# Fewer, larger loads per pair of heads, with GpSimd placing the last 64 tokens, and the first weights on ScalarE's queue

## The chip, the core and the metric

The kernel runs on one core of one Trainium2 chip. The metric is the device time of one execution in microseconds (us). Of the kernel before there are three timed executions: median 894.34 us, from 890.95 to 898.97. One more execution was profiled; all rows below come from it.

## The reference

Eight batches of 576 tokens pass through three blocks.

```python
# attention with a feature map, per head (8 heads of 64)
def phi(x):
    proj = x @ w_phi                                   # 64 -> 128
    proj = proj - max(abs(proj), axis=-1)
    return concatenate([exp(proj), exp(-proj)])        # 256 features
kv = phi(k).T @ v;  z = sum(phi(k), tokens)
x  = (phi(q) @ kv) / (phi(q) @ z + 1e-6)               # heads side by side: 576 x 512
# causal convolution of 5 taps, gate, two products
gate = sigmoid(conv5(x));  x = (gate * (x @ w_val)) @ w_outA
# gated MLP with a product over tokens
h = relu(x @ w_in);  u, v = h[:, :512], h[:, 512:]
v = layernorm(v);  v = w_spatial @ v + b_spatial
out = (u * v) @ w_out
```

The moe weights w_val, conv_w, w_out and w_out2 are given as 64-bit floats; the kernel loads their two 32-bit words and puts them together itself. It multiplies w_outA by w_in once (the product weights wg and wu), and splits each operand of the large products into a high and a low part, so that one product is three matmuls.

## The kernel before, in words

The program is not written out in the order in which it runs. Each operation is recorded with a key (a place in time, L33 to L36), the buffers it reads and writes, and the engines that may do it. A planner in the kernel (`order`, L222) then plays the engines in a model of its own and writes out an instruction order for each engine: at each moment an engine takes the ready operation with the smallest key. A key may run ahead of the oldest unfinished one by at most WINDOW, 0.405. Buffers come from an arena in SBUF (`fa`, 19152 columns; `ra` for the split operands) and are reused; where a buffer is reused, the instruction that fills it waits for the last user of what lay there. On the chip nothing of the model's times remains: each engine and each queue runs its instructions in the order written, and stops at an instruction whose semaphores have not come.

Work units around the change:

- **Weights** (`weights`, L516). POOL (GpSimd) writes zeros and ones into small tiles, then runs one partition_all_reduce on a tile `warm`. An identity matrix is made in DRAM: `eye` is filled with zeros, then its diagonal with ones, then read back into `ident`. Each 128 rows of a 64-bit weight take one transfer of 512 KB, an absolute value on ScalarE (ACT), four operations on VectorE (DVE) and, for w_val, a copy (ACT) and a subtraction (DVE).
- **A pair of heads** (32 pairs, `attention`, L744). `load_k` and `load_q` (L591, L605) load 512 tokens of k, q and v into arena buffers, and the last 64 tokens of both heads into block-diagonal tiles `k4`, `q4` and `v4` (three of each, used in turn). `project` (L616) makes 12 products on TensorE (PE). `kexp` (DVE, ACT) makes the features of k; `qmax` copies the projected q out of PSUM (ACT) and takes its maximum over partitions (POOL, partition_all_reduce); `kvacc` makes k-features times v, `kvturn` transposes it with `ident`, `num` multiplies by q's features (24 products of 32x288 and those of the denominator), and `divide` (L729) sends the denominators through DRAM (`rden`) and multiplies.
- **A batch** (`mlp`, L788). When the four pairs of a batch are divided, the convolution, the split and the product with `wv` (w_val) begin; `wg`, `wu`, `ws` and `wo` follow.

All transfers are issued by SP (SyncE), in one queue (`dma`, L422). A transfer takes one of eight semaphores in turn, and waits for the transfer that used that semaphore before. Every operation helper has one line (L383 for ACT and DVE, L418 POOL, L428 transfers, L439 and L452 products, L673 transposes), so the rows are told apart by tile names: `fa` is the arena, `ra` the split operands, `bank` PSUM.

Of the kernel before, what the change touches and what calls it, by code (L numbers as in the profile page):

```python
# [12 lines left out]
U32 = mybir.dt.uint32  # L13
# [6 lines left out]
B, H, S, D = 8, 8, 576, 64  # L20
F = 128
DM = 512
# [3 lines left out]
REM = 512  # L26
# [8 lines left out]
W_VAL, W_CONV, W_OUT, W_G, W_U, W_SP, W_OUT2, W_STEP, W_EYE = -1.59, -1.198, -0.852, -0.889, -0.626, -0.225, 0.273, 0.06, -1.334  # L35
M_CONV, M_VAL, M_V, M_U, M_SP, M_OUT, M_ALL = -0.177, -0.295, -0.048, 0.078, 0.002, 0.205, 57.899  # L36
LONG_W, LONG_A, LONG_M = True, False, False
WINDOW = 0.405
# [118 lines left out]
class Op:  # L157
    __slots__ = ("key", "ways", "bufs", "need", "users", "ready", "start", "end", "way", "n", "modes")

# [29 lines left out]
class Plan:  # L189
# [7 lines left out]

    def add(self, ways, reads, writes, modes=(FULL, FULL)):

# [3 lines left out]
        op.key = self.key  # L203
        op.modes = modes
        op.users, op.ready, op.start, op.end, op.way = [], 0.0, None, None, None
# [16 lines left out]
    def order(self, window, hold):  # L222
# [41 lines left out]
        while len(done) < len(ops):  # L264
# [13 lines left out]
            while again:  # L278
# [4 lines left out]
                for e in self.ENGINES:  # L283
# [6 lines left out]
                    for op in ready:  # L290
# [4 lines left out]
                        if e == "PE":  # L295
# [4 lines left out]
                            busy = op.end - now  # L300
                        if e == "SP":
                            transfers = max(transfers, now + busy + 0.63) + until
                            op.end = transfers + 0.85
# [34 lines left out]
def attn_moe_gmlp_kernel(  # L338
# [82 lines left out]

    def dma(out, in_):  # L422
        n = 1
        for d in (out.shape() if isinstance(out, View) else out.shape):
            n *= d

        def run():
            nc.sync.dma_start(out=real(out), in_=real(in_))  # L428

        rows = (out.shape() if isinstance(out, View) else out.shape)[0]  # L430
        plan.add({"SP": (0.475 if rows == 128 else 0.65, 4 * n / 360e3, run)}, views(in_), views(out))

# [27 lines left out]
    def split(src, hi, lo):  # L460

        copy(hi, src)
        sub(lo, src, hi.f32())
# [28 lines left out]

    def load_f64(src, n):

        raw, w = fa.buf(2 * n), fa.buf(n)
        m = 2 * n // len(src)
        for i, x in enumerate(src):
            dma(raw.bitcast(U32)[:, m * i:m * i + m], x.bitcast(U32))
        words = raw.bitcast(U32).rearrange("p (n t) -> p n t", t=2)
# [13 lines left out]
    def rows(ap, k):  # L513
        return ap[128 * k:128 * k + 128]

    def weights():  # L516
# [6 lines left out]
        def fill(x, value):  # L523
            pool(0.1 + cols_of(x) / 960, "memset", x, [], x, value)


        for t in k4 + q4 + v4:
            for hh in range(2):
                fill(t[64 * hh:64 * hh + 64, 64 - 64 * hh:128 - 64 * hh], 0.0)
# [5 lines left out]
        fill(warm, 0.0)  # L535
        pool(9.0, "partition_all_reduce", warm[:, 4:8], [warm], warm[:, 4:8], warm[:, 0:4], channels=128,
             reduce_op=bass_isa.ReduceOp.absmax)
        at(W_EYE)
        zero, one = fa.buf(128), fa.buf(1)
        fill(zero, 0.0)  # L540
        dma(eye, zero)
        fill(one, 1.0)
        dma(eye.rearrange("a b -> (a b)")[0:128 * 128:129].unsqueeze(1), one)
        dma(ident, eye)
# [44 lines left out]
    xt = {}  # L589

    def load_k(P):  # L591
# [21 lines left out]
    def half(hh):  # L613
        return slice(64 * hh, 64 * hh + 64)

    def project(k, kl, q, ql):  # L616
# [6 lines left out]
            for c in range(4) for hh in range(2)  # L623
        ] + [(qas[hh], wphi[half(hh)], q[half(hh)], True, True) for hh in range(2)], FULL, ROWS)
        return kas + [rest[:, 0:F]], [(qas[hh], rest[:, F + 64 * hh:F + 64 * hh + 64]) for hh in range(2)]
# [378 lines left out]
```

## Time and profile before

| | |
|---|---|
| timed executions | 890.95, 894.34, 898.97 us |
| the profiled execution | 895.74 us |
| its span, first to last instruction | 894.0 us |
| PE busy | 846.4 us, 95% |
| DVE, ACT, POOL busy | 694.3, 515.0, 148.1 us |
| mean granted clock of TensorE | 0.988 |
| share of the chain of waits | PE 69%, DVE 13%, DMA 11% |

The span is 1.7 us less than the execution's time. A busy share is a mean over stages; the rows below cut the span where the work changes. A "granted clock" of 1.00 is 2.4 GHz, the other level is 1.2 GHz, and a value between them is a mix of both in that stretch.

### The profile page before, as it was taken

Reading aid. Unit: us, or ns where it says so; the run is one execution under the profiler, and the core shown is the slowest. Engines: PE = TensorE matmul, PEld = TensorE weight load, DVE = VectorE, ACT = ScalarE, POOL = GpSimd, SP = SyncE. Lnnn points to the kernel's source line nnn. Section 1 sums busy time; section 2 is a strip of 40 time slices with the busy share of each in tenths; the row PEclk is TensorE's granted clock in tenths of the full one; section 3 lists DMA queues with packets and bytes.
Section 4 is the critical chain, followed back from the end, with each engine's and each line's share of the span. In section 5 each row is a group of like instructions: output and inputs, shape, how many; then the busy total and the mean of one; then the engine's idle time right before and its main releaser. Section 6 shows DMA issues by size and latency. Waiting matters only on the chain.

```text
span 894.0 us, 19046 instructions
## 1 busy us (share of the span) xinstructions
PE 846.4 (95%) x7312; PEld 671.4 (75%) x7312; DVE 694.3 (78%) x1619; ACT 515.0 (58%) x1097; POOL 148.1 (17%) x129
## 2 busy tenths in 40 slices
PE   3769889899999999999999999999999999999997
PEld 2534468677886887777887888787887888789896
DVE  5888778997877897688778896688878896796541
ACT  3856565575566664576566664576556674543331
POOL 4421210211211120111111120112211110100000
PEclk8999989999999999999999999999999999999999
DMA  5764215130221313131221222130221221010001
GB/s 184 226 180 120 68 27 178 27 88 27 77 66 43 74 38 102 42 89 27 64 81 42 75 65 78 41 88 26 72 73 43 74 65 38 13 46 27 24 7 59
DMA packets 66131, 62.22 MB, mean 70 GB/s; under 512 B 28662, under 2 KB 45430, under 8 KB 66040
## 3 DMA queue, kind: packets, MB, share of 16 engines
q1 hardware_dynamic: 66040, 61.00, 24.3%
q8 instruction: 57, 0.93, 0.4%
q14 instruction: 34, 0.28, 0.1%
HBM read 50.13 MB, written 9.65 MB: 67 GB/s over the span
## 4 chain that ended last, share of the span: by engine, by line
PE 69%; DVE 13%; DMA 11%; ACT 3%; issue 2%; SPq 2%; POOL 0%; DVEq 0%; ACTq 0%; POOLq 0%
PE bank L439 48%; PE bank L452 20%; DVE fa L383 11%; DMA fa<-rden 5%; ACT fa L383 3%; SPq L428 2%; DVE ra L383 1%; DMA fa<-in_w_spT_dram 1%; PE bank L673 1%; DMA rden<-fa 1%; DMA fa<-in_w_out_dram 1%; DMA fa<-in_v_dram 1%; DMA fa<-in_w_val_dram 1%; DMA k<-in_kT_dram 0%; POOL fa L418 0%
## 5 line engine op out<-in xcount | busy, mean ns | idle before, releaser
L383 ACT ACTIVATE fa<-fa 128x576 f32<-128x576 f32 (+2 forms) x445 | 255.1, 628 | 104.6 <-DVE fa L383 72.8
L383 ACT ACTIVATE fa<-bank 128x512 f32<-128x512 f32 (+6 forms) x395 | 162.1, 455 | 162.7 <-PE bank L439 85.6
L418 POOL PARTITION_ALL_REDUCE fa<-fa x64 | 140.6, 2237 | 528.1 <-ACT fa L383 405.1
L383 DVE TENSOR_TENSOR fa<-fa 128x576 f32<-128x576 f32 (+4 forms) x348 | 157.1, 465 | 57.6 <-DMA fa<-rden 29.6
L452 PE MATMUL bank<-fa 128*32 128x288 f32 (+2 forms) x2192 | 164.0, 402 | 3.0 <-DVE fa L383 1.1
L452 PEld LDWEIGHTS bank<-fa 128*32 128x32 f32 (+1 forms) x2192 | 76.0, 112 | 78.2 <-issue 30.7
L383 ACT ACTIVATE ra<-fa 128x256 fp32r<-128x256 f32 (+5 forms) x201 | 87.1, 459 | 82.4 <-DVE fa L383 69.0
L439 PE MATMUL bank<-ws,ra 128*128 128x256 f32 (+1 forms) x768 | 114.7, 298 | 2.5 <-DVE fa L383 2.0
L439 PE MATMUL bank<-wg,ra 128*128 128x512 f32 (+1 forms) x480 | 116.4, 395 | 0.0
L439 PE MATMUL bank<-ra,wu 128*128 128x256 f32 (+1 forms) x768 | 111.6, 301 | 4.9 <-DVE fa L383 3.4
L439 PEld LDWEIGHTS bank<-ra,wu 128*128 128x128 f32 x768 | 105.0, 191 | 13.0 <-issue 5.2
L383 DVE TENSOR_TENSOR ra<-fa,ra 128x256 fp32r<-128x256 f32 (+4 forms) x224 | 103.1, 488 | 13.0 <-ACT ra L383 5.9
L439 PEld LDWEIGHTS bank<-ws,ra 128*128 128x128 f32 x768 | 104.9, 189 | 7.2 <-DVE fa L383 4.2
L439 PEld LDWEIGHTS bank<-ra,wv 128*128 128x128 f32 x768 | 103.0, 189 | 8.5 <-ACT fa L383 4.0
L439 PE MATMUL bank<-ra,wv 128*128 128x256 f32 (+1 forms) x768 | 105.8, 297 | 2.2 <-ACT fa L383 2.2
L383 DVE SCALAR_TENSOR_TENSOR fa<-fa,convw 128x576 f32<-128x576 f32 x128 | 102.9, 823 | 2.4 <-ACT fa L383 2.0
L439 PEld LDWEIGHTS bank<-wg,ra 128*128 128x128 f32 (+1 forms) x480 | 83.7, 179 | 25.7 <-DVE fa L383 1.9
L439 PE MATMUL bank<-wo,ra 128*128 128x512 f32 x432 | 101.6, 391 | 0.2 <-DVE fa L383 0.2
L383 DVE SCALAR_TENSOR_TENSOR fa<-fa 128x576 f32<-128x576 f32 (+4 forms) x192 | 93.8, 496 | 9.1 <-ACT fa L383 6.8
L439 PEld LDWEIGHTS bank<-wo,ra 128*128 128x128 f32 x432 | 80.4, 188 | 18.0 <-issue 0.9
L383 DVE TENSOR_SCALAR fa<-fa 128x2 int32<-128x2 int32 (+8 forms) x192 | 51.3, 284 | 20.1 <-ACT fa L383 14.4
L383 DVE TENSOR_REDUCE fa<-bank 128x4 f32<-128x512 f32 (+1 forms) x96 | 51.0, 548 | 16.3 <-PE bank L452 14.0
(63 smaller groups left out, 614.3 us busy)
## 6 DMA issues: line engine op xcount, KB each, us to landing
fa<-rden SPq DMA_DIRECT2D x64, 144.0 KB
fa<-in_v_dram SPq DMA_DIRECT2D x32, 264.0 KB
fa<-in_qT_dram SPq DMA_DIRECT2D x32, 256.0 KB
fa<-in_kT_dram SPq DMA_DIRECT2D x32, 256.0 KB
out_dram<-fa SPq DMA_DIRECT2D x32, 256.0 KB
fa<-in_w_in_dram SPq DMA_DIRECT2D x8, 512.0 KB
fa<-in_w_val_dram SPq DMA_DIRECT2D x4, 512.0 KB
fa<-in_w_outT_dram SPq DMA_DIRECT2D x4, 512.0 KB
```

What stands on the lines that cost most here:

```text
L383: return lambda: getattr(engine, method)(**{k: real(v) for k, v in kw.items()})
L418: getattr(nc.gpsimd, method)(*(real(a) for a in args), **{k: real(v) for k, v in kw.items()})
L428: nc.sync.dma_start(out=real(out), in_=real(in_))
L439: nc.tensor.matmul(real(acc), lhsT=real(l), rhs=real(r), start=first and i == 0, stop=last and i == n - 1)
L452: nc.tensor.matmul(real(o), lhsT=real(l), rhs=real(r), start=first, stop=last)
L673: nc.tensor.transpose(real(tp)[:, F * s:F * s + F], real(kvT)[:, F * s:F * s + F], real(ident))
```

## The change

Per pair, SP now issues four transfers instead of nine: q whole (576 tokens), k whole, v of 512 tokens, and v's last 64 tokens once for both halves of the partitions (`vt`, a broadcast). Six copies of 64x64 on POOL (`place`) put the last tokens into `k4`, `q4` and `v4`. The buffers of k and q grow from 512 to 576 columns. The four transfers of w_val and the three of `eye` and `ident` go to ACT's queue. The fills of POOL stand in another order, with the tiles of pair 0 and `warm` first. Eleven keys have other values, and attention's buffers are taken from the upper end of the arena (LONG_A).

```diff
-AK_LOAD, AK_PROJ, AK_ACC, AK_SUM, AK_TURN = -0.401, 0.095, 0.584, 0.308, 2.416
-AQ_LOAD, AQ_MAX, AQ_EXP, AQ_NUM, AQ_HEAD, A_DIV = -0.902, 0.399, 1.995, 3.059, 1.055, 5.005
+AK_LOAD, AK_PROJ, AK_ACC, AK_SUM, AK_TURN = -0.44, 0.095, 0.595, 0.308, 2.337
+AQ_LOAD, AQ_MAX, AQ_EXP, AQ_NUM, AQ_HEAD, A_DIV = -0.852, 0.399, 2.005, 3.059, 1.055, 5.031
...
-LONG_W, LONG_A, LONG_M = True, False, False
+LONG_W, LONG_A, LONG_M = True, True, False
...
-    def dma(out, in_):
+    def dma(out, in_, engine="SP"):
...
-            nc.sync.dma_start(out=real(out), in_=real(in_))
+            (nc.sync if engine == "SP" else nc.scalar).dma_start(out=real(out), in_=real(in_))
...
+        zero, one = fa.buf(128), fa.buf(1)
+        fill(zero, 0.0)
+        fill(one, 1.0)
+        for i in range(3):
+            for t in (k4[i], q4[i], v4[i]):
+                for hh in range(2):
+                    fill(t[64 * hh:64 * hh + 64, 64 - 64 * hh:128 - 64 * hh], 0.0)
+            if not i:
+                fill(warm, 0.0)
+                at(-1.99)
+                pool(9.0, "partition_all_reduce", warm[:, 4:8], [warm], warm[:, 4:8], warm[:, 0:4], channels=128,
+                     reduce_op=bass_isa.ReduceOp.absmax)
...
-        dma(eye, zero)
+        dma(eye, zero, "ACT")
...
-            split(load_f64([rows(w_val, k)], DM), wv[0][k], wv[1][k])
+            split(load_f64([rows(w_val, k)], DM, "ACT"), wv[0][k], wv[1][k])
...
+    def place(out, in_):
+        pool(0.2, "tensor_copy", out, [in_], out, in_)
+
     def load_k(P):
         b, hp = divmod(P, NP)
-        k = fa.buf(REM)
-        dma(k, kT[b, hp, :, 0:REM])
+        k, vt = fa.buf(S), fa.buf(2 * VW)
+        dma(k, kT[b, hp, :, 0:S])
         v = fa.buf(4 * 2 * VW)
         dma(v.rearrange("p (c d) -> p c d", c=4), v1[b, 0:REM, hp].rearrange("(c p) d -> p c d", p=128))
+        dma(vt, v1[b, REM:S, hp].unsqueeze(0).to_broadcast([2, 64, 2 * VW]))
         kl, vl = k4[P % 3], v4[P % 3]
         for hh in range(2):
-            r = slice(64 * hh, 64 * hh + 64)
-            dma(kl[r, r], kT[b, hp, r, REM:S])
-            dma(vl[r, r], v1[b, REM:S, hp, (2 * VW - D) * hh:(2 * VW - D) * hh + D])
+            r = half(hh)
+            place(kl[r, r], k[r, REM:S])
+            place(vl[r, r], vt[r, (2 * VW - D) * hh:(2 * VW - D) * hh + D])
...
     def load_q(P):
         b, hp = divmod(P, NP)
-        q, ql = fa.buf(REM), q4[P % 3]
-        dma(q, qT[b, hp, :, 0:REM])
+        q, ql = fa.buf(S), q4[P % 3]
+        dma(q, qT[b, hp])
         for hh in range(2):
-            dma(ql[half(hh), half(hh)], qT[b, hp, half(hh), REM:S])
+            place(ql[half(hh), half(hh)], q[half(hh), REM:S])
```

What the planner makes of it stands in the order of the built programs. The engines' first instructions are the first place. SP, before (the loads of pair 0; `k_0`, `q_0`, `v_0` are its block-diagonal tiles; DMAHW is another transfer's semaphore):

```order
L428 DMA wphi<-in_w_phi_dram 128x1x128
L428 DMA fa<-in_qT_dram 128x512
L428 DMA q_0_82<-in_qT_dram 64x64 x2
L428 DMA fa<-in_w_val_dram 128x1024
L428 DMA fa<-in_kT_dram 128x512
L428 DMA fa<-in_v_dram 128x4x132
L428 DMA k_0_79<-in_kT_dram 64x64
```

and SP, changed:

```order
L428 DMA wphi<-in_w_phi_dram 128x1x128
L428 DMA fa<-in_qT_dram 128x576
L428 DMA fa<-in_kT_dram 128x576 [waits DVE_49]
L428 DMA fa<-in_v_dram 128x4x132
L428 DMA fa<-in_v_dram 128x1x132
L428 DMA fa<-in_qT_dram 128x576 [waits DMAHW0_49]
L428 DMA fa<-in_kT_dram 128x576 [waits DMAHW2_49]
```

The load of k of pair 0 has been given columns that the first block of w_val used; the value it waits for is DVE's fifth instruction, the subtraction that ends that block. Everything of SP after it, the loads of v and of pair 1 among them, stands behind it.

ACT, changed (before, no transfer stood here: the table load was followed by the absolute value and the copy `wv_0`, and the first copies of `bank_70` and `bank_67` were its fifth and sixth ACTIVATE):

```order
L428 DMA fa<-in_w_val_dram 128x1024
L383 ACT_TABLE_LOAD
L383 ACTIVATE fa<-fa 128x512 [waits DMAHW0_49]
L383 ACTIVATE wv_0_99<-fa 128x512 [waits DVE_49]
L428 DMA fa<-in_w_val_dram 128x1024 [waits Activation_49]
L428 DMA fa<-in_w_val_dram 128x1024
L428 DMA fa<-in_w_val_dram 128x1024 [waits DMAHW1_49]
L428 DMA eye<-fa 128x128 [waits DMAHW3_49,Pool_49]
L428 DMA eye<-fa 128x1 [waits DMAHW3_49,DMAHW0_49,Pool_49]
L383 ACTIVATE fa<-fa 128x512
```

The last row is the absolute value of the second block of w_val. It now stands behind two transfers of `eye`: the first waits until the second block of w_val has landed, the second until the first has landed in DRAM and until q of pair 1 has landed. On POOL, the copies into `k_0` wait for the load of k.

The second place is PE ahead of the first product with `wv` (batch 0). Before, the end of pair 5's kvacc, the products of `num` of pair 4, a transpose, and then `wv`:

```order
L452 MATMUL bank_67<-fa,v_2_87 128x256
L452 MATMUL bank_67<-fa 32x256 x16
L452 MATMUL bank_67<-fa,ones 32x128 x4
L452 MATMUL bank_67<-fa,mine_89 32x128 x2
L452 MATMUL bank_67<-fa,mine_90 32x128 x2
L452 MATMUL bank_70<-fa 32x288 x8
L452 MATMUL bank_71<-fa 32x288 x8
L452 MATMUL bank_73<-fa 32x288 x8
L673 MATMUL bank_67<-ident,fa 128x128 x3
L439 MATMUL bank_67<-ra,wv_0_99 128x256
```

Changed, `num` of pair 3 (the last that batch 0 needs), with kvacc of pair 4 and the last weight products (128x512) behind it; after these come only the 12 products of pair 5's projection, and then `wv`:

```order
L452 MATMUL bank_68<-fa 32x288 x8
L452 MATMUL bank_71<-fa 32x288 x8
L452 MATMUL bank_73<-fa 32x288 x8
L452 MATMUL bank_69<-fa 128x512 x4
L452 MATMUL bank_67<-fa,v_1_86 128x256
L452 MATMUL bank_67<-fa 32x256 x16
L452 MATMUL bank_67<-fa,ones 32x128 x16
L452 MATMUL bank_67<-fa,mine_89 32x128 x2
L452 MATMUL bank_67<-fa,mine_90 32x128 x2
L452 MATMUL bank_69<-fa 128x512 x4
L452 MATMUL bank_67<-fa 128x512 x4
L452 MATMUL bank_68<-fa 128x512 x4
```

Counted in the built programs: before, 464 products of PE stand ahead of the first with `wv`, now 397; `num` of pair 3 stood behind 147 DVE instructions, now behind 114; the first `wv` product behind 168, now 158. At PE's 661st product both orders stand at the same place, the third group of `wu` of batch 0; 233 DVE instructions are needed for it before, 223 now, and 238 for the group of `wg` behind it.

## Rows read from the trace of the kernel before

**Rows 1.** Windows: stretch, us, busy PE, PEld, DVE, ACT, POOL, PEclk, DMA share, GB/s

```profile
0.00:20.00 20.00, 4.37 (x25) 3.32 (x26) 10.24 (x15) 6.71 (x12) 10.20 (x35) 0.91 0.64 201
20.00:64.00 44.00, 32.47 (x448) 19.57 (x449) 38.56 (x70) 30.14 (x69) 14.32 (x8) 0.93 0.67 192
64.00:108.00 44.00, 43.07 (x307) 21.67 (x310) 38.26 (x68) 26.50 (x54) 8.55 (x6) 1.00 0.38 108
108.00:160.00 52.00, 41.88 (x378) 33.13 (x369) 40.23 (x87) 30.82 (x66) 9.39 (x7) 0.93 0.31 91
...
200.00:889.00 689.00, 685.57 (x5795) 565.33 (x5794) 529.74 (x1286) 392.16 (x838) 101.23 (x70) 1.00 0.20 54
```

**Rows 2.** Waits of PE, first 160 us: us in total, times, longest

```profile
PE bank L452 <- DMA k<-in_kT_dram: 15.6, 2, 9.5
```

**Rows 3.** Timeline of SP's queue: start, us, what [idle before, releaser]

```profile
3.18 0.58 SPq L428 DMA_DIRECT2D fa<-in_w_val_dram  x1
...
5.96 0.59 SPq L428 DMA_DIRECT2D k<-in_kT_dram  x1
...
7.23 1.53 SPq L428 DMA_DIRECT2D fa<-in_w_val_dram  x3
...
14.48 3.20 SPq L428 DMA_DIRECT2D eye<-fa  x2
17.73 0.47 SPq L428 DMA_DIRECT2D k<-in_kT_dram  x1
```

**Rows 4.** Chain of waits within the first 30 us: start, us, what

```profile
7.23 4.57 DMA fa<-in_w_val_dram
```

**Rows 5.** Waits of SP's queue, first 30 us

```profile
SPq L428 <- DMA eye<-fa: 2.5, 1, 2.5
```

**Rows 6.** Timeline of ACT

```profile
7.07 0.66 ACT L383 ACTIVATE fa<-fa 128x512 f32<-128x512 f32 x1 [5.06 <-DMA fa<-in_w_val_dram]
...
13.81 1.32 ACT L383 ACTIVATE fa<-bank 128x512 f32<-128x512 f32 x4
```

**Rows 7.** Timeline of DVE

```profile
7.76 0.89 DVE L383 TENSOR_SCALAR fa<-fa 128x512 f32<-128x512 f32 x2 [7.76 <-ACT fa L383]
...
10.80 0.69 DVE L383 TENSOR_TENSOR wv<-fa,wv 128x512 fp32r<-128x512 f32 x1 [0.70 <-ACT wv L383]
12.59 0.89 DVE L383 TENSOR_SCALAR fa<-fa 128x512 f32<-128x512 f32 x2 [1.09 <-ACT fa L383]
...
15.06 1.52 DVE L383 TENSOR_SCALAR fa<-fa 128x512 uint32<-128x512 uint32 x1
...
19.40 1.27 DVE L383 TENSOR_REDUCE fa<-bank 128x4 f32<-128x512 f32 x2
...
112.79 0.69 DVE L383 TENSOR_TENSOR fa<-fa 128x512 f32<-128x512 f32 x1 [4.74 <-ACT fa L383]
```

**Rows 8.** Groups of POOL by shape: busy us, mean ns of one, idle before

```profile
L418 POOL PARTITION_ALL_REDUCE fa<-fa x64 | 140.6, 2237 | 528.1 <-ACT fa L383 405.1 <-DVE fa L383 76.4 <-DMA out_dram<-fa 17.7
...
L418 POOL MEMSET k<- 64x64 f32 x6 | 0.9, 146 | 0.5 <-POOLq L988 0.3
```

**Rows 9.** Timeline of PE

```profile
9.53 0.77 PE L452 MATMUL bank<-wphi,k 128*128 128x128 f32 x2 [9.53 <-DMA k<-in_kT_dram]
...
19.86 0.77 PE L452 MATMUL bank<-wphi,k 128*128 128x128 f32 x2 [6.10 <-DMA k<-in_kT_dram]
...
25.65 0.67 PE L452 MATMUL bank<-fa,v 128*128 128x256 f32 x2 [1.61 <-issue]
...
63.84 7.10 PE L452 MATMUL bank<-fa 128*128 128x512 f32 x16 [1.08 <-DVE fa L383]
...
105.45 3.09 PE L452 MATMUL bank<-fa 128*32 128x288 f32 x48
...
127.33 11.30 PE L439 MATMUL bank<-ra,wv 128*128 128x256 f32 x84 [2.04 <-ACT fa L383]
...
159.26 2.56 PE L439 MATMUL bank<-ra,wu 128*128 128x256 f32 x12 [2.28 <-DVE fa L383]
```

More of the change, by code (lines that the diff above doesn't have):

```diff
@@ L157 @@
 class Op:
-    __slots__ = ("key", "ways", "bufs", "need", "users", "ready", "start", "end", "way", "n", "modes")
+    __slots__ = ("key", "ways", "bufs", "need", "users", "ready", "start", "end", "way", "n", "modes", "dma")
 def cols_of(x):
@@ L196, in __init__, with add @@
         self.key = 0.0
-    def add(self, ways, reads, writes, modes=(FULL, FULL)):
+    def add(self, ways, reads, writes, modes=(FULL, FULL), dma=False):
         op = Op()
@@ L203, in add @@
         op.key = self.key
-        op.modes = modes
+        op.modes, op.dma = modes, dma
         op.users, op.ready, op.start, op.end, op.way = [], 0.0, None, None, None
@@ L427, in run @@
         def run():
-            nc.sync.dma_start(out=real(out), in_=real(in_))
+            (nc.sync if engine == "SP" else nc.scalar).dma_start(out=real(out), in_=real(in_))
         rows = (out.shape() if isinstance(out, View) else out.shape)[0]
-        plan.add({"SP": (0.475 if rows == 128 else 0.65, 4 * n / 360e3, run)}, views(in_), views(out))
+        plan.add({engine: (0.475 if rows == 128 else 0.65, 4 * n / 360e3, run)}, views(in_), views(out), dma=True)
     def gemm(acc, terms, first=True, last=True):
@@ L490, in attn_moe_gmlp_kernel, with load_f64 @@
     ws = wtiles("ws", 4, S)
-    def load_f64(src, n):
+    def load_f64(src, n, engine="SP"):
         raw, w = fa.buf(2 * n), fa.buf(n)
@@ L524, in fill @@
             pool(0.1 + cols_of(x) / 960, "memset", x, [], x, value)
-        for t in k4 + q4 + v4:
-            for hh in range(2):
-                fill(t[64 * hh:64 * hh + 64, 64 - 64 * hh:128 - 64 * hh], 0.0)
+        zero, one = fa.buf(128), fa.buf(1)
[10 more added lines that the diff above has]
+                     reduce_op=bass_isa.ReduceOp.absmax)
         fill(ones, 1.0)
@@ L533, in weights @@
                 fill(mine[hh][64 * r:64 * r + 64], float(r == hh))
-        fill(warm, 0.0)
-        pool(9.0, "partition_all_reduce", warm[:, 4:8], [warm], warm[:, 4:8], warm[:, 0:4], channels=128,
-             reduce_op=bass_isa.ReduceOp.absmax)
         at(W_EYE)
-        zero, one = fa.buf(128), fa.buf(1)
-        fill(zero, 0.0)
-        dma(eye, zero)
-        fill(one, 1.0)
-        dma(eye.rearrange("a b -> (a b)")[0:128 * 128:129].unsqueeze(1), one)
-        dma(ident, eye)
+        dma(eye, zero, "ACT")
+        dma(eye.rearrange("a b -> (a b)")[0:128 * 128:129].unsqueeze(1), one, "ACT")
+        dma(ident, eye, "ACT")
         for x, value in ((s2, 1.0), (wr2, 0.0)):
@@ L589, in attn_moe_gmlp_kernel, with half @@
     xt = {}
+    def half(hh):
+        return slice(64 * hh, 64 * hh + 64)
+    def place(out, in_):
+        pool(0.2, "tensor_copy", out, [in_], out, in_)
     def load_k(P):
         b, hp = divmod(P, NP)
-        k = fa.buf(REM)
-        dma(k, kT[b, hp, :, 0:REM])
+        k, vt = fa.buf(S), fa.buf(2 * VW)
+        dma(k, kT[b, hp, :, 0:S])
         v = fa.buf(4 * 2 * VW)
         dma(v.rearrange("p (c d) -> p c d", c=4), v1[b, 0:REM, hp].rearrange("(c p) d -> p c d", p=128))
+        dma(vt, v1[b, REM:S, hp].unsqueeze(0).to_broadcast([2, 64, 2 * VW]))
         kl, vl = k4[P % 3], v4[P % 3]
         for hh in range(2):
-            r = slice(64 * hh, 64 * hh + 64)
-            dma(kl[r, r], kT[b, hp, r, REM:S])
-            dma(vl[r, r], v1[b, REM:S, hp, (2 * VW - D) * hh:(2 * VW - D) * hh + D])
+            r = half(hh)
+            place(kl[r, r], k[r, REM:S])
+            place(vl[r, r], vt[r, (2 * VW - D) * hh:(2 * VW - D) * hh + D])
         return k, v, kl, vl
@@ L623, in project @@
             for c in range(4) for hh in range(2)
-        ] + [(qas[hh], wphi[half(hh)], q[half(hh)], True, True) for hh in range(2)], FULL, ROWS)
+        ] + [(qas[hh], wphi[half(hh)], q[half(hh), 0:REM], True, True) for hh in range(2)], FULL, ROWS)
         return kas + [rest[:, 0:F]], [(qas[hh], rest[:, F + 64 * hh:F + 64 * hh + 64]) for hh in range(2)]
```

10 lines of the change are left out of this document (4 added, 6 removed).

## The prediction, made before the changed kernel ran

> **What bounds the kernel now.** I read the windows first, cut where the work changes [rows 1]. From 200 to 889 us PE is busy 685.57 of 689.0 us at clock 1.00: this stage is PE's, and an edit to loads or small copies can gain at most 3.4 us there. PE's idle time lies in the first 160 us: 15.6 us in the first 20, 11.5 in the next 44, 0.9 to 108 and 10.1 to 160, 38.2 us in all. The change can only win or lose in this stage, and its worth is read at the point where PE no longer waits. That is the start of `wu`'s third group at 159.26 us, its last wait of over 1 us [rows 9]. If PE gets there earlier by some time, the end comes earlier by as much.
>
> What holds PE up before that point is read from the rows of the queues. PE's first product waits 9.53 us and pair 1's 6.10 more, both for small loads of k [rows 2, 9]. The second was late because SP stood at the two `eye` transfers from 14.48 us and issued the second half of `k_1` only at 17.73 [rows 3], 2.5 us of it a wait for the first `eye` transfer to land [rows 5]. From 20 us on DVE sets the pace: it is busy 38.56 of 44.0 us while PE is at 32.47 [rows 1]. At 112.79 DVE itself stood 4.74 us [rows 7], behind the division of the last pair that batch 0 needs, and PE reached the first `wv` product at 127.33 [rows 9].
>
> **The change, part by part.**
>
> *The five small transfers per pair.* Each takes SP 0.5 to 0.6 us (0.59 for one of `k` [rows 3]), so 160 of them are some 90 us of SP's time. After 200 us this buys nothing, since PE waits there 3.4 us in all. In the first 20 us it would bring pair 1 forward, were SP free.
>
> *SP is not free.* Its third transfer, k of pair 0, now waits for DVE's fifth instruction. I work out when that ends. The first block of w_val was issued at 3.18 [rows 3] and used at 7.07 [rows 6]: 3.89 us. ACT now issues it at SP's former start, about 0.7, so it is used at 4.6. The fifth instruction ended at 10.80 + 0.69 = 11.49 [rows 7], 4.42 us after that use. So k of pair 0 is issued at 9.0, where it was 3.8. A landing costs 3.57 us (5.96 to 9.53 [rows 3, 9]) or, with w_val under way, 4.57 [rows 4]: k lands between 12.6 and 13.6. The two copies on POOL are not in this trace; the fill of the same 64x64 took 0.146 us [rows 8], a bound from below, and I take 0.3 each. PE's first product then starts near 13.5, 4 us later than now.
>
> *ACT's queue.* The other three blocks of w_val are issued behind the copy of the first, 3.7 us after its landing, at 8.3. The second block lands at 8.3 + 4.57 = 12.9. Only then ACT issues the first `eye` transfer; the next waits 2.5 us for its landing, so at least until 15.8, and for q of pair 1, which is the fourth load behind k. From 8.3 on some 2.5 MB stand ahead of that one in both queues, which at the 201 GB/s of the first window [rows 1] take until 20.7. Between 15.8 and 20.7 I take 17.5: the two queues share the transfers, and half of w_val may come after. The absolute value of the second block is queued behind it, and DVE's sixth instruction starts near 18.6, where it started at 12.59 [rows 7]. DVE is idle from 9.0 to there. This is the wait that takes the place of the one removed: what was SP's stop for `eye` is now ACT's, and DVE, the pace-setter, stands behind it.
>
> *The lag it leaves.* Before, nine DVE instructions from 12.59 to 19.40 (6.8 us) led up to pair 0's `kexp` [rows 7], one of them, at 15.06, stretched to 1.52 us while POOL's first all-reduce ran; its like take 0.45 (0.89 for two). Now thirteen lead up to it. At about 0.6 each without that stretch they take 7.9 us, so `kexp` starts at 26.5. Of the four added, 2.2 us are work taken from later. The lag is 26.5 - 19.4 - 2.2 = 4.9 us, from 3 (`eye` at 15.8) to 8 (at 20.7). Of the 5.4 us that DVE idles from 20 to 64 us [rows 1], I let the lag use up 2 (0 to 3), as the loads it waited for will have come.
>
> *The copies on POOL.* 192 in all, about 30 before 64 us. POOL has room: 148 of 894 us, plus 192 x 0.3 = 58. In the DVE-paced stage the question is whether they hold up DVE. The stretched instruction at 15.06 shows that POOL's all-reduce, 2.24 us long [rows 8], held DVE about 1.1 us, half its length. By that row 30 copies of 0.15 to 0.3 us hold DVE for 2 to 5 us if all meet it, and for nothing if none does. I take 1.5. The Trainium skill, "SBUF — State Buffer", section "Who interferes with whom", says that a DVE instruction with two SBUF inputs contends with a GpSimd instruction that reads SBUF, and that whichever starts second is blocked for the other's whole length. The row agrees that there is blocking, though for less than the whole length; by the rule alone the copies would cost up to 9 us at 0.3 each, or 7.5 more than I take, and the time would be near 900.
>
> The lag at the weight products is then 4.9 - 2 + 1.5 = 4.4 us.
>
> *The other order.* Before, DVE had 83 instructions behind it when PE began the weight products at 63.84 and 147 at `num` of pair 3 at 105.45 [rows 9]: 0.65 us each. From there to `wv` it was 21 instructions in 21.9 us, since the division of pair 3 had to be waited for. In the changed order `num` of pair 3 needs 114 instructions instead of 147, and `wv` 158 instead of 168, so the division runs while DVE has other work. At 0.65 us each, instruction 158 falls at 63.84 + 75 x 0.65 + 4.4 = 117.0 us, 10.3 us before the old 127.33. But PE has then done 67 products fewer. Before, 196 products of this stretch took 31.9 us less two waits of 0.87 and 2.28: 0.147 each. The 264 now take 38.8, and I add 1.7 us for waits (1 to 3). PE reaches product 661 at 157.5, where it was 159.26: 1.8 us earlier. DVE allows it: 65 more instructions at the 0.49 us they took there (31.9/65) end at 149.
>
> *Behind 160 us* POOL gets about 170 copies. DVE has 159 us to spare in 689; I cost them at nothing, since PE's products cover them, and at up to 5 us if a late `k4` or a held DVE shows where PE has no stock of work.
>
> Sum: 894.0 - 1.8 = 892.2 us of span, 893.9 with the 1.7 outside it. The profiled execution (895.74) lies 1.4 over the median of the runs; 894.34 - 1.8 gives **892.5**. Its own range: the lag from 1 to 9.5 us and the waits move it from 888 to 898; with the 5 us behind 160, to 902.
>
> **Rivals.**
>
> *The lag stays.* If DVE and not PE paces all of the first 160 us, no order helps: the lag of 4.9 us plus the copies' 2 to 5, less nothing, with PE reaching product 661 at 167. It decides if DVE has no idle stretch like that at 112.79 left to give. For it: DVE busy 38 of 44 us in two windows [rows 1]. Against: 11.8 us idle in the third. With 1 to 4 us behind 160: +8 to +12, **904**. Chance 0.16.
>
> *The waits of the third stage all go.* `wv` early enough would leave neither the 4.74 us stop nor PE's 10.1 us of idle time between 108 and 160, and the slow clock there (0.93 on average, PE restarting after long idle) would be full. If the lag is at its lower end and absorbed, the end comes 8 to 12 us earlier, **884**. For it: `num` of pair 3 stands 33 DVE instructions earlier. Against: all of PE's first 26 us lie later. Chance 0.22.
>
> *The order shows a wait that the chip doesn't meet.* If q of pair 1 and `eye` land quickly, DVE's stop ends at 15.8 and the lag is 3; that is in the forecast's range, near 890.
>
> **How the numbers follow.** Forecast 0.62, lag 0.16, waits gone 0.22. A measurement here tells 1% (9 us) from no change: below 885.4 is faster, above 903.3 slower. Of the third case's 0.22 about two thirds falls below 885.4, and 0.06 of the forecast's lower tail with it: faster 0.21. Of the lag's 0.16 two thirds lies above 903.3, and 0.03 of the forecast with the copies dear: slower 0.14. Same 0.65. The range leaves out some 0.1 at each end: 883 to 903.
>
> **What would show each step.** In the changed profile: k's load of pair 0 issued at 8.5 to 9.5 and PE's first product at 12.5 to 14; DVE idle from about 9 to 16 or later, with ACT's absolute value released by an `eye` transfer; 192 COPY rows on POOL of 0.15 to 0.3 us; `wv` first at 112 to 122; product 661 (third `wu` group) at 153 to 162; PE over 99% busy after 200 us. The prediction is wrong if DVE's stop is much shorter or longer, if the copies take 0.5 us or more, if `wv` still waits for the division, or if PE's idle time behind 200 us grows beyond 5 us.

## The result, and the profile after

The changed kernel takes 901.45 us (median of 20 executions, 898.68 to 904.5); beside it the kernel before took 893.75 (20 executions). The ratio is 1.0081, with a 95% interval from 1.0066 to 1.0096. The change costs 0.8%, where 0.2% of gain was forecast. Its profiled execution took 902.21 us, with a span of 900.4.

Windows of the changed kernel, columns as in [rows 1]:

```profile
0.00:20.00 20.00, 4.19 (x24) 3.14 (x24) 3.95 (x8) 3.81 (x5) 7.69 (x43) 1.00 0.62 205
20.00:64.00 44.00, 30.48 (x399) 18.32 (x399) 37.04 (x73) 29.29 (x67) 21.70 (x26) 0.87 0.53 158
64.00:108.00 44.00, 40.45 (x319) 19.64 (x319) 37.99 (x65) 24.19 (x52) 16.47 (x20) 0.94 0.46 143
108.00:160.00 52.00, 45.59 (x358) 33.53 (x362) 43.36 (x88) 31.99 (x67) 11.91 (x14) 0.97 0.28 82
...
200.00:889.00 689.00, 682.15 (x5786) 562.72 (x5786) 541.44 (x1302) 390.60 (x828) 150.64 (x202) 1.00 0.19 55
```

DVE was busy 10.24 us in the first window before, now 3.95. From 200 to 889 us PE stands idle 6.85 us, where it was 3.4. Of the 6.4 us by which the span grew, 4.6 have come together by product 661 (the third group of `wu`), at some 160 us. Timeline of SP's queue after:

```profile
8.72 0.33 SPq L428 DMA_DIRECT2D fa<-in_kT_dram  x1
...
102.91 4.99 SPq L428 DMA_DIRECT2D fa<-in_w_spT_dram  x2
107.99 0.73 SPq L428 DMA_DIRECT2D fa<-in_b_sp_dram  x2
109.95 0.34 SPq L428 DMA_DIRECT2D rden<-fa  x1
```

Timeline of ACT after; the bracket is the idle time before a group and who ended it:

```profile
7.34 1.31 ACTq L428 DMA_DIRECT2D fa<-in_w_val_dram  x3
11.03 7.16 ACTq L428 DMA_DIRECT2D eye<-fa  x2
18.24 1.24 ACT L383 ACTIVATE fa<-fa 128x512 f32<-128x512 f32 x2 [10.27 <-DMA fa<-in_qT_dram]
```

Timeline of DVE after (the answers to [rows 7]):

```profile
18.95 0.89 DVE L383 TENSOR_SCALAR fa<-fa 128x512 f32<-128x512 f32 x2 [10.26 <-ACT fa L383]
...
26.65 1.28 DVE L383 TENSOR_REDUCE fa<-bank 128x4 f32<-128x512 f32 x2
...
50.51 0.76 DVE L383 TENSOR_TENSOR fa<-fa 128x576 f32<-128x576 f32 x1 [3.13 <-POOL fa L418]
```

Timeline of POOL after:

```profile
14.47 0.51 POOL L418 COPY k<-fa 64x64 f32<-64x64 f32 x2 [5.82 <-DMA fa<-in_kT_dram]
...
48.18 0.23 POOL L418 COPY v<-fa 64x64 f32<-64x64 f32 x1 [2.27 <-DMA fa<-in_v_dram]
48.39 2.08 POOL L418 PARTITION_ALL_REDUCE fa<-fa  x1
```

Timeline of PE after (the answers to [rows 9]):

```profile
15.03 0.80 PE L452 MATMUL bank<-wphi,k 128*128 128x128 f32 x2 [15.03 <-POOL k L418]
...
32.39 1.22 PE L452 MATMUL bank<-fa,v 128*128 128x256 f32 x2 [4.33 <-ACT fa L383]
...
123.88 7.52 PE L439 MATMUL bank<-ra,wv 128*128 128x256 f32 x48 [2.56 <-DVE wu L383]
...
163.81 1.68 PE L439 MATMUL bank<-ra,wu 128*128 128x256 f32 x12
```

Up to DVE's `kexp` at 26.65 nearly everything stands where it was forecast: k's load at 8.72, ACT's stop of 7.16 us at the two `eye` transfers, DVE idle for 10.26 us; only PE's first product is late, at 15.03 for 13.5. Then a thing comes that the forecast did not have: POOL stops at a copy of v whose load has not landed, the all-reduce of q's maximum stands behind this copy, and DVE waits 3.13 us for the all-reduce. PE reaches `wv` at 123.88 (before 127.33, forecast 117.0) and product 661 at 163.81 (before 159.26, forecast 157.5). Groups of POOL by shape after, columns as in [rows 8]:

```profile
L418 POOL PARTITION_ALL_REDUCE fa<-fa x64 | 141.0, 2246 | 187.8 <-ACT fa L383 100.5 <-DVE fa L383 49.2 <-DVE ra L383 17.5
L418 POOL COPY q<-fa 64x64 f32<-64x64 f32 x64 | 26.2, 410 | 109.6 <-DMA fa<-in_qT_dram 100.7 <-DVE fa L383 7.2
L418 POOL COPY k<-fa 64x64 f32<-64x64 f32 x64 | 25.5, 399 | 106.8 <-DMA fa<-in_kT_dram 92.7 <-DVE ra L383 12.0 <-issue 0.2
L418 POOL COPY v<-fa 64x64 f32<-64x64 f32 x64 | 23.1, 361 | 83.0 <-DMA fa<-in_v_dram 76.3 <-DVE fa L383 5.1
```

The copies take 74.8 us in all, 0.36 to 0.41 each on average. The column behind tells more: at these copies POOL stood 269.7 us waiting for loads, and whatever followed them in its queue stood with it. The sum is no price: in a kernel below that is 0.8% faster (v by direct transfers) the copies of k and q alone stand 230.9 us so.

### The profile page after: what moved, and what is told of

Same layout as the page of the kernel before. It is cut to its first block, busy times and chain, and to the rows that moved or that the text cites. A ratio compares the mean times of both kernels' runs of the same rounds, so it can differ in the third digit from the quotient of the medians.

```text
span 900.4 us, 19132 instructions
## 1 busy us (share of the span) xinstructions
PE 848.7 (94%) x7312; PEld 671.4 (75%) x7312; DVE 702.0 (78%) x1632; ACT 512.3 (57%) x1084; POOL 222.4 (25%) x321
## 5 line engine op out<-in xcount | busy, mean ns | idle before, releaser
L383 ACT ACTIVATE fa<-fa 128x576 f32<-128x576 f32 (+3 forms) x448 | 260.4, 631 | 121.5 <-DVE fa L383 85.8
L383 ACT ACTIVATE fa<-bank 128x512 f32<-128x512 f32 (+6 forms) x385 | 158.2, 456 | 156.4 <-PE bank L439 84.3
L383 DVE TENSOR_TENSOR fa<-fa 128x576 f32<-128x576 f32 (+4 forms) x348 | 162.2, 481 | 48.7 <-DMA fa<-rden 26.2
L452 PE MATMUL bank<-fa 128*32 128x288 f32 (+2 forms) x2192 | 167.7, 408 | 7.8 <-ACT fa L383 7.8
L383 ACT ACTIVATE ra<-fa 128x256 fp32r<-128x256 f32 (+6 forms) x200 | 86.6, 462 | 83.5 <-DVE fa L383 71.5
L383 DVE TENSOR_TENSOR ra<-fa,ra 128x256 fp32r<-128x256 f32 (+4 forms) x224 | 105.4, 501 | 12.5 <-ACT ra L383 5.1
L383 DVE SCALAR_TENSOR_TENSOR fa<-fa,convw 128x576 f32<-128x576 f32 x128 | 105.5, 838 | 4.4 <-ACT fa L383 3.9
L383 DVE SCALAR_TENSOR_TENSOR fa<-fa 128x576 f32<-128x576 f32 (+4 forms) x192 | 90.2, 480 | 12.4 <-ACT fa L383 10.1
L383 DVE TENSOR_SCALAR fa<-fa 128x512 f32<-128x512 f32 (+8 forms) x189 | 46.9, 265 | 24.6 <-ACT fa L383 18.9
```

Of the source, the lines that this page charges most:

```text
L383: return lambda: getattr(engine, method)(**{k: real(v) for k, v in kw.items()})
L452: nc.tensor.matmul(real(o), lhsT=real(l), rhs=real(r), start=first, stop=last)
```

## The experiments

Ratios are to the kernel before, with their 95% intervals; that of the change itself is 1.0081. "Start mended" means the edit of the third experiment. Short diffs are against the changed kernel, or against the kernel named.

### The start: k's load, or ACT's stop?

**k's load freed of its wait.** After planning, k of pair 0 gets columns of its own:

```diff
+        k, load = self.k0
+        k.at = (0, k.at[1])
```

> The changed kernel with one difference: k of pair 0 is given columns that nothing has used, so its load is the third on SP's queue without a wait; order and all other places are the changed kernel's. Theory START (what was lost is PE's and DVE's late start): k issued near 2.0 instead of 8.72, PE's first product at 6 to 8 instead of 15.03; q of pair 1 lands earlier, so ACT's stop at eye ends 2 to 4 us before 18.24; the end 2 to 4 us before the changed kernel's, 897.5 to 899.5. Theory COPIES (GpSimd's copies hold DVE and stand before its all-reduces): within 1 us of 901.5. Theory ORDER (the other keys cost it, whatever starts first): within 1.5 us of 901.5.

Measured 1.0141 (1.0123 to 1.0159), slower than the change. Timelines of ACT and of PE in this kernel:

```profile
10.34 4.98 ACTq L431 DMA_DIRECT2D fa<-in_w_val_dram  x3
15.42 6.57 ACTq L431 DMA_DIRECT2D eye<-fa  x2
22.04 1.22 ACT L386 ACTIVATE fa<-fa 128x512 f32<-128x512 f32 x2 [14.06 <-DMA eye<-fa]
```

```profile
9.26 0.80 PE L455 MATMUL bank<-wphi,k 128*128 128x128 f32 x2 [9.26 <-POOL k L421]
...
36.17 1.22 PE L455 MATMUL bank<-fa,v 128*128 128x256 f32 x2 [4.33 <-ACT fa L386]
```

PE's first product comes 5.8 us earlier and its kvacc 3.8 us later. SP's loads now go out ahead of ACT's transfers, which wait longer: ACT's `eye` stop ends at 22.0 instead of 18.2, and DVE goes on at 22.73. ACT's stop paces the start, and as long as it stands, PE's first product is worth nothing.

**The three `eye` transfers later.** They are issued ahead of ACT's operations 17, 24 and 32, counted from 0, from tiles that stay:

```diff
+        done = [o for o in done if o not in self.eye]
+        for o, i in zip(self.eye, (17, 24, 32)):
+            done.insert(done.index(acts[i]), o)
```

> The changed kernel with one difference: the three transfers of eye and ident stand later on ACT's queue (behind the copies of q of pair 0, of pair 1, and before the first conv weights' copy), and the zeros and ones they read have tiles of their own. k of pair 0 still waits. START: DVE's restart at 12.5 to 14 instead of 18.95 (landing of w_val's second block 12.9 or before), the first kvacc at 27 to 29 instead of 32.39, the end 2 to 5 us earlier, 896.5 to 899.5. COPIES and ORDER: first kvacc earlier too, but the end within 1.5 us of 901.5.

Measured 1.0051 (1.0035 to 1.0067). DVE in this kernel:

```profile
11.80 0.89 DVE L390 TENSOR_SCALAR fa<-fa 128x512 f32<-128x512 f32 x2 [3.06 <-ACT fa L390]
...
25.98 0.69 DVE L390 TENSOR_TENSOR fa<-bank,fa 128x512 f32<-128x512 f32 x1 [5.11 <-PE bank L459]
```

DVE restarts at 11.80 instead of 18.95; 5.11 us of that are lost again to k's late load, and PE's kvacc comes at 28.91, 3.5 us earlier. The end comes 2.9 us earlier.

**Start mended.** Both edits together, and the blocks of w_val issued one behind the other, the second into columns of its own:

```diff
+        k.at = (0, k.at[1])
+        raws[1].bufs[0].at = (36, 64)
+        for o in raws[:0:-1]:
+            done.remove(o)
+            done.insert(done.index(raws[0]) + 1, o)
```

> The changed kernel with three differences at its start, the rest of the order as it is: k of pair 0 in unused columns (no wait), w_val's other three blocks issued right behind its first on ACT's queue, and the three transfers of eye and ident later on ACT's queue. Theory ACT STOP (DVE's restart behind ACT's stop sets the start, and a shift of the start reaches the end nearly whole: 3.8 us later there gave 2.6 to 5 later at the end with k free): first kvacc at 23 to 26 instead of 32.39, the end 5 to 8 us earlier than the changed kernel, 891 to 894 against 891.75 before. Theory ORDER (the other keys hold more than half of the loss): the shift at the first kvacc is used up by 160 us, the end no earlier than 896.

Measured 1.0058 (1.0036 to 1.008). PE's kvacc starts at 29.13, where 23 to 26 was expected, and `wv` at 119.69 instead of 123.88. ACT in this kernel:

```profile
0.73 9.27 ACTq L443 DMA_DIRECT2D fa<-in_w_val_dram  x4
...
11.32 0.66 ACT L398 ACTIVATE fa<-fa 128x512 f32<-128x512 f32 x1
```

So the start is better and not free of stops: ACT's stop at `eye` is gone, but the fourth transfer of w_val now waits until a load of q on SP's queue has landed, at 9.64, and ACT's first operation stands behind it (11.32, where it was 4.24 in the change). A start without either stop was not built. Of the loss, 0.6% is still there; the next experiments show that not all of it is the start's.

### The copies: how much?

**Copies left out from pair 3 on, or all of them three times each:**

```diff
+            for _ in range(1 if P < 3 else 0):      # the other kernel: range(3)
+                nc.gpsimd.tensor_copy(real(out), real(in_))
```

> The changed kernel with GpSimd's copies left out from pair 3 on (174 of 192; the last 64 tokens of those pairs keep what pairs 0 to 2 left); order and places are unchanged. COPIES: DVE's busy sum falls by some 7 us (701.98 to about 695), PE's idle time behind 200 us from 6.85 to about 3.5, all-reduces no longer stand behind a load of v (2.27 us at 48.18); the end 4 to 6 us earlier, 895.5 to 897.5. START: the end within 1.5 us of 901.5, since the first 60 us keep 18 copies. ORDER: PE's idle time behind 200 us stays near 6.9 and the end within 1.5 us of 901.5.

> The changed kernel with each of the 192 copies on GpSimd issued three times in a row; order and places are unchanged. COPIES: 384 more copies of 0.26 to 0.41 us add 10 to 16 us to DVE's busy sum and the end comes 4 to 10 us later, 905.5 to 911.5. START and ORDER: DVE's hold is covered behind 200 us, the end less than 2 us later, 901.5 to 903.5.

Without copies 1.0038 (1.002 to 1.0056), with three of each 1.0362 (1.034 to 1.0384): the first set costs 0.43%, the two added sets 2.8% more. DVE's busy time is the same with copies and without (702.0 and 701.9 us), so at the change's number of copies DVE does not get longer, it waits. With three of each it is 707.7, 5.7 us more for 384 added copies, of some 24 us of loss. The waits of PE with three copies (us in total, times, longest; the change has one, of 15.0):

```profile
PE bank L452 <- POOL k L600: 24.3, 3, 16.2
```

**The same, start mended:**

> The start mended as in the kernel before, and GpSimd's copies left out from pair 3 on (174 of 192; those pairs keep what pairs 0 to 2 left in the blocks). If the two losses are apart and add up: 3 to 5 us earlier than the mended start alone, ratio 0.993 to 0.998 to the kernel before. If they are one (both only let DVE run earlier up to the same next wait): within 1.5 us of the mended start alone.

Measured 0.9955 (0.9935 to 0.9975), against 1.0058 with the copies: 1.0% for them with the mended start.

### The copies: whose?

**v's last tokens by two direct transfers**, the copies of k and q as in the change:

```diff
-        dma(vt, v1[b, REM:S, hp].unsqueeze(0).to_broadcast([2, 64, 2 * VW]))
-            place(vl[r, r], vt[r, (2 * VW - D) * hh:(2 * VW - D) * hh + D])
+                nc.sync.dma_start(out=real(vl[r, r]), in_=v1[b, REM:S, hp, (2 * VW - D) * hh:(2 * VW - D) * hh + D])
```

> The changed kernel with one difference: the last 64 tokens of v come by two transfers straight into the blocks, without the broadcast and the two copies; the start is not mended. If the copies of v are the whole price of the 192 copies: as without copies, ratio 1.001 to 1.005 against 1.0081. If the three kinds of copies share it: 1.006.

> The mended start, and the last 64 tokens of v come by two transfers straight into the blocks instead of one broadcast and two copies: five transfers a pair and 128 copies instead of 192; places and order are otherwise the same. IN ORDER (7 of the 10 all-reduces that started right behind a copy stood behind one of v): most of the 9 us between the mended start and the mended start without copies: ratio 0.996 to 1.001. OCCUPANCY: a third of it, 1.001 to 1.004. If SP's time is scarce, no gain.

Without the mended start 0.9999 (0.9981 to 1.0017); with it 0.9956 (0.994 to 0.9973), 887.38 us, faster than both kernels, and nothing is left out of it. With the start mended, leaving out all copies (0.9955) or v's copies and broadcast load (0.9956) is the same. Four views of the kernel without the mended start, POOL, DVE, SP and PE:

```profile
45.23 0.25 POOL L419 COPY k<-fa 64x64 f32<-64x64 f32 x1
45.44 2.29 POOL L419 PARTITION_ALL_REDUCE fa<-fa  x1
```

```profile
47.93 0.78 DVE L384 TENSOR_TENSOR fa<-fa 128x576 f32<-128x576 f32 x1
```

```profile
100.42 1.18 SPq L429 DMA_DIRECT2D fa<-in_w_spT_dram  x2
...
104.15 0.35 SPq L429 DMA_DIRECT2D rden<-fa  x1
```

```profile
117.72 7.49 PE L440 MATMUL bank<-ra,wv 128*128 128x256 f32 x48 [1.23 <-DVE wu L384]
...
157.62 1.68 PE L440 MATMUL bank<-ra,wu 128*128 128x256 f32 x12
```

The same all-reduce starts at 45.44 instead of 48.39, and the same DVE instruction at 47.93, without a wait, instead of 50.51. Read instruction by instruction, the changed kernel's DVE lags this one by 2.6 us from there, by 3.4 at 101.7, and by 5.8 from 109.0 on. This second step does not come through the order of POOL's queue. POOL, ACT and DVE in the changed kernel:

```profile
104.80 1.22 POOL L418 COPY v<-fa 64x64 f32<-64x64 f32 x2 [4.04 <-DMA fa<-in_v_dram]
```

```profile
106.05 1.26 ACT L383 ACTIVATE fa<-fa 128x576 f32<-128x576 f32 x2 [4.38 <-DVE fa L383]
```

```profile
108.99 0.82 DVE L383 SCALAR_TENSOR_TENSOR fa<-fa,convw 128x576 f32<-128x576 f32 x1 [2.28 <-ACT fa L383]
```

and the same ACT instruction without copies, and with v direct:

```profile
103.04 1.26 ACT L383 ACTIVATE fa<-fa 128x576 f32<-128x576 f32 x2 [3.23 <-DMA fa<-in_v_dram]
```

```profile
98.71 1.26 ACT L384 ACTIVATE fa<-fa 128x576 f32<-128x576 f32 x2 [0.48 <-DMA fa<-fa]
```

In the changed kernel ACT starts as the copy of v ends (104.80 + 1.22); the view names DVE, but POOL's semaphore is among those that ACT waits for, and with v direct it is not. Without copies ACT waits for a load of v instead. So this instruction fills columns in which the broadcast tile `vt` lies until it has been copied (inferred from these three releases; the traces show no addresses). SP's stop of 4.99 us at w_spT (here 1.18) ends behind the same ACT instruction. At `wv` the lag is 6.2 us, of 7.6 at the end. ACT stands so once more behind 200 us, 3.23 us for a copy of v until 300.89, and the next row is PE's behind it:

```profile
301.65 1.57 PE L439 MATMUL bank<-ws,ra 128*128 128x256 f32 x11 [1.41 <-ACT fa L383]
```

This kernel also drops the broadcast load of v, which copies_out keeps. With the start mended the two ways agree (0.9955 and 0.9956). But one keeps the broadcast load and the other the copies of k and q, so this shows that these two cost about the same, and not that each costs nothing; no kernel has neither the load nor the copies of k and q and yet the merged loads. Without the mended start the two ways are 1.0038 and 0.9999, with spans of 893.4 and 892.8 us, and copies_out still stops 3.84 us at w_spT. That part of v's price is therefore not shown to be the copies': up to 0.4% of the 0.8% may come with the broadcast load in this one order.

**Nine transfers and no copies, with the new order and the mended start:**

```diff
+            nc.sync.dma_start(out=real(k), in_=kT[b, hp, :, 0:S])
+            for hh in range(2):
+                nc.sync.dma_start(out=real(kl[half(hh), half(hh)]), in_=kT[b, hp, half(hh), REM:S])
```

> The mended start with no copies: k, q and v each have two transfers of 64x64 straight into the blocks again, nine transfers a pair, in the changed kernel's order and places. What the merged loads of k and q bring: if SP's time matters in the first 130 us, 2 to 5 us later than with v alone direct (0.9956), ratio 0.998 to 1.002; if it does not, 0.994 to 0.997.

Measured 1.0009 (0.9993 to 1.0025): the merged loads of k and q gain 0.5% (1.0009 to 0.9956); the new order with the mended start gains nothing over the order before.

### v's copies: by waiting, by running, or by their place?

**All copies without a load to wait for:** from pair 3 on they read weights that lie in SBUF, so k4, q4 and v4 hold other data.

```diff
+            nc.gpsimd.tensor_copy(real(out), real(in_ if P < 3 else wphi[half(hh), 0:64]))
```

> The changed kernel with all 192 copies on GpSimd, but from pair 3 on each reads the same rows of wphi instead of the loads of k, q and v: the copies run, and wait for no load (the blocks of those pairs then hold w_phi instead of the last 64 tokens). Theory IN ORDER (a copy that waits for its load keeps the all-reduce behind it): as without copies, ratio 1.002 to 1.006. Theory OCCUPANCY (running 192 copies beside DVE is the price): as the changed kernel, ratio 1.007 to 1.010.

> The mended start with all copies; from pair 3 on the copies of v read rows of wphi, so they run but wait for no load (the blocks of v then hold w_phi instead of the last 64 tokens). If a copy's wait for its load with an all-reduce behind it is the whole price of v's copies: ratio 0.994 to 0.998, as with v's direct transfers (0.9956). If running them, or the broadcast load, has its own price: 1.000 to 1.005, as with the late copies (1.0029).

Measured 1.0057 (1.0037 to 1.0078) for all copies; with the start mended and v's copies alone 1.0002 (0.9983 to 1.0021). The latter stands in the middle between v's copies as they are (1.0058) and none (0.9956): about half of the price goes with what the copies read, that is, with the wait for the load and with the hold that a copy keeps on the columns of `vt`.

**Spare copies in their place.** Start mended, v by direct transfers, and 58 copies where v's copies stood, on which nothing depends:

```diff
+                if P >= 3:
+                    nc.gpsimd.tensor_copy(real(plan.still[0][1][r, 0:64]), real(wphi[r, 0:64]))
```

> Start mended and v's last tokens loaded by two direct transfers (as in the kernel that measured 0.9956), and in the places of v's copies in GpSimd's order, from pair 3 on, 58 spare copies of 64x64 that read weights and write a tile that nobody reads: no load is waited for and no product waits for them, but GpSimd's queue is as long as with v's copies. Theory 'running': a copy costs by taking GpSimd's time and its port in front of the all-reduces, so the half of v's price that is left without the load's wait comes back: 0.999 to 1.002. Rival 'dependence': that half comes from the products that wait for their copy of v at the end of GpSimd's queue: 0.994 to 0.998, as without copies of v.

Measured 0.9943 (0.9924 to 0.9962). Running costs nothing that can be measured. From 200 to 800 us, the windows of the change, of mended with v direct, and of this kernel:

```profile
200.00:800.00 600.00, 593.15 (x5202) 480.98 (x5205) 488.74 (x1157) 359.39 (x765) 150.64 (x202) 1.00 0.21 60
```

```profile
200.00:800.00 600.00, 597.93 (x5258) 486.51 (x5257) 494.50 (x1170) 360.88 (x770) 134.04 (x154) 1.00 0.21 59
```

```profile
200.00:800.00 600.00, 597.87 (x5255) 487.03 (x5255) 495.72 (x1168) 361.53 (x771) 151.64 (x196) 1.00 0.21 59
```

POOL (fifth pair) is as busy with spare copies as in the change, 151.64 against 150.64 us, and PE stands idle 2.13 us instead of 6.85 (6.50 with the mended start alone). The other half of v's price stays open. Two things could hold it. One is a dependence: the product with `v4` waits for its copy, and the copy for the products that read `v4` before. The trace of the kernel whose copies of v wait for no load speaks against it: there no product of PE is held by a copy of v, and no copy of v by PE. The other is the broadcast load, which that kernel keeps and the one with spare copies does not.

**Copies moved behind the all-reduce that follows them:** 42 of k, q and v, and, with the start mended, 17 of v alone.

```diff
+                if o.way == "POOL" and o.ways["POOL"][0] > 1.0:
+                    to = x
+            if to:
+                done.insert(to, done.pop(i))
```

> The changed kernel with the same 192 copies, but 42 of them stand behind the next one or two all-reduces on GpSimd's queue instead of before them, where the planner had both within 3 us; all else as it is. Theory IN ORDER (the copies cost because an all-reduce that DVE and PE need stands behind a copy that waits for its load, 10 places with waits of 2 to 6 us): most of the 3.8 us of the kernel without copies, so 2 to 4 us earlier than the changed kernel: ratio 1.004 to 1.006. Theory OCCUPANCY (each copy costs by running): no change, ratio 1.007 to 1.009. If a product then waits for its own late copy, later than that.

> The mended start, and 17 of the copies of v stand behind the next all-reduce on GpSimd's queue instead of before it; no copy of k or q is moved (moving those made PE wait 7.84 us at pair 1). IN ORDER: ratio 0.997 to 1.002 against 1.0058 of the mended start. OCCUPANCY: 1.004 to 1.008.

The first measured 1.0133 (1.0112 to 1.0155), worse than the change. PE in that kernel:

```profile
27.96 0.80 PE L469 MATMUL bank<-wphi,k 128*128 128x128 f32 x2 [7.84 <-POOL k L435]
```

The queue works both ways: now PE's projection waits 7.84 us for a copy of k behind an all-reduce. With v's copies alone 1.0029 (1.0009 to 1.0048) against 1.0058 (1.0036 to 1.008): 0.3% of the 1.0% may be won by their place alone, though the intervals overlap.

### The old order

**The kernel before with only the four loads and the copies; the same with v direct; and the kernel before with only the new keys.**

> The kernel before with the four transfers a pair and GpSimd's copies alone: old keys, old fill order, all transfers on SP, old arena ends. On SP 5 small transfers of pair 0 go and eye moves behind pair 1's loads. Theory ACT STOP: no stop of ACT, so no loss at the start, pair 1 earlier (second projection before 19.86), and the copies' in-order cost of some 3.8 us remains: ratio 0.996 to 1.004. Theory TRANSFERS (the merged loads and copies are the loss by themselves): ratio 1.006 to 1.010. A new order by the planner elsewhere can add 2 us either way.

> The kernel before with merged loads of k and q, their copies on GpSimd, and v's last tokens by two direct transfers; keys, fills and queue as before. It was 1.0139 with v's copies too. If v's copies are the price in this order as well: 0.997 to 1.004. If the planner's other order or the copies of k (PE waited 9.4 us for them after the first) are: 1.008 or more.

> The kernel before with the changed kernel's eleven keys and arena ends alone: nine transfers a pair, no copies, all on SP, old fill order. If the new order gains some 6 us, as forecast before the lag is taken off: ratio 0.991 to 0.997. If the order is what lost: 1.003 or more. The planner writes a new order for it, so 2 us either way say nothing.

Measured 1.0139 (1.0116 to 1.0163), 1.0038 (1.0017 to 1.0059) and 1.0224 (1.0199 to 1.0248). In the old order v's way through POOL, copies and broadcast load, costs 1.0% too. The new keys with the old transfers are the worst of the three; PE in that kernel:

```profile
103.51 2.07 PE L452 MATMUL bank<-fa 128*128 128x512 f32 x2 [6.61 <-DVE fa L383]
...
138.46 1.22 PE L452 MATMUL bank<-fa,v 128*128 128x256 f32 x2 [8.02 <-ACT fa L383]
```

An order's keys fit the transfers that they were made with, and can't be priced apart from them.

## Why the prediction was wrong

The sum by runs, from the kernel before: new order and mended start with nine transfers +0.1%; merged loads of k and q -0.5%; ACT's stop at the start +0.4%; v through POOL, copies and broadcast load, +0.8%. Each is a difference of two ratios above, and they hold for this sequence: taken the other way round, with v's copies still there, mending the start gives 0.2% and v costs 1.0%. "ACT's stop" is what the mended start gives back; ACT's stop of 9.27 us in it is still to be won.

**The step that failed: the copies on POOL, "I take 1.5".** Ahead of 160 us the step asked only whether the running copies hold DVE, and bounded that by 0 to 5 us; behind 160 it allowed 5 for a late `k4` or a held DVE. DVE's busy time is the same with them and without (702.0 and 701.9 us). Yet v's copies with their broadcast load cost 6.2 us at `wv` and 7.6 at the end, in two ways that the traces show. One is what stands behind a waiting copy in POOL's order (DVE's 3.13 us at 50.51): ten all-reduces in the changed kernel start directly behind a copy, seven of them behind one of v, and v_direct has four. The other is what waits for the columns of `vt` (ACT's 4.38 us at 106.05). With the mended start about half of the price remains when the copies wait for no load, and what holds that half is open. [Rows 8] held the hint: 64 all-reduces, which DVE waits for, on an engine that had little else queued. The prediction named what is queued behind ACT's and SP's stops and did not do so for POOL.

The Trainium skill, "PSUM — Partial Sum Buffer", section "Engine vs sequencer instructions", says that GpSimd's queue is strict FIFO, as those of ACT and DVE are. The trace agrees: the all-reduce at 48.39 stood behind a copy that waited 2.27 us for a load it had nothing to do with. This rule should have been in the forecast, not the port rule. That one, the Trainium skill's "SBUF — State Buffer", section "Who interferes with whom", would have the later of two instructions blocked; the copies' mean of 0.36 to 0.41 us, where more than half take 0.23 to 0.27, agrees with it on POOL's side, while DVE's equal busy time shows no such block. (The row that the prediction held beside it, at 15.06, is a TENSOR_SCALAR with one tensor input, and did not test it.) The time near 900 that the prediction worked out from it was met by luck.

**The steps that held.** k's load was issued at 8.72 (9.0 forecast). DVE went on at 18.95 (18.6), released by ACT behind the `eye` transfers and the load of q. `kexp` came at 26.65 (26.5). The load itself landed later than I took, so PE's first product came at 15.03 (13.5), which k0_free shows to matter nothing while ACT's stop stands. The other order is the step with the longest working: with v's way through POOL taken out, v_direct has `wv` at 117.72 (117.0) and product 661 at 157.62 (157.5), and takes 892.46 us (892.5). That it meets the forecast to a tenth is partly luck: v_direct is another kernel than the one forecast, and beside the kernel before its ratio is 0.9999 (0.9981 to 1.0017), where 892.5 of 894.34 is 0.998.

**Behind 160 us** the copies were costed at nothing to 5 us; PE's idle time behind 200 us rose by 3.4 us. Of the 8.2 us by which the span missed the forecast (900.4 to 892.2), 6.3 stood at product 661 (163.81 to 157.5) and 1.9 came behind it.

**The signs.** Of the signs that the prediction named, five came out against it: PE's first product (15.03), the length of a copy (0.36 to 0.41 us on average), `wv` (123.88), product 661 (163.81), and PE's idle time behind 200 us, which grew beyond 5 us. The measured 901.45 us lies inside the stated range, at the end kept for dear copies and a lag that stays.

**The rivals.** The lag-stays case gave 904 with product 661 at 167; the measured time is nearest to it, but its mechanism is not the one: DVE was held by a queue and by a buffer, and with v's copies and broadcast load gone product 661 comes where it was forecast. The waits-all-gone case is what mended_v_direct comes close to, 887.38 us against 884; it needed the mended start and v's way through POOL gone. The case in which the chip does not meet ACT's stop did not happen.

## What to carry to other kernels

Price an instruction that is added to an in-order engine by what it waits for and by who waits for the instruction behind it, not by its length or by how idle the engine is: POOL was as busy with the spare copies (0.9943) as in the change (1.0081). A copy that replaces a transfer moves the wait for a load from a queue where little depends on the next entry to one where the pace-setter's next input stands. It also keeps the loaded buffer until it has run: ask who gets those columns next. And a transfer on a compute engine's queue stops that engine until the semaphores it waits for have come: 7.16 us for two `eye` transfers of little data, 9.27 us for four of w_val at the mended start.

## What was not expected of the hardware

- Loads issued earlier on SP's queue slowed ACT's: with k's load freed, three transfers of w_val took ACT 4.98 us to issue from 10.34 on, instead of 1.31 from 7.34, and the first 36 us became 3.8 us longer. In the trace the second of the three went out at 14.49, as a load of v on SP's queue landed; transfers on both queues take the same eight semaphores in turn. An earlier start on one queue can be a later end of both.
- The small write of `rden` issued at 109.95, behind two loads of w_spT and two of b_sp, kept SP waiting 6.0 us for its landing. The same write did so with v direct (from 104.15 to 110.54). Why was not tried.
- The all-reduce on the tile `warm` took 0.385 us, where the planner's model gives it 9.0. What that number did to the order of the start was not tried.
